# Attention feeding eight routed experts on one core: expert pieces one half-block earlier, the tail's transpose in its own batch, masks and GpSimd fills in another order

## The chip, the core and the metric

The kernel runs on one core of a Trainium2 chip. The core has a matrix engine (PE, with its weight loads counted apart as PEld), a vector engine (DVE), a scalar engine (ACT), GpSimd (POOL) and a queue engine (SP) that issues transfers; POOL issues some transfers too. Each engine takes its instructions in the order in which the program gives them and waits at each for what it reads. The metric is the time of one execution in microseconds (us) on the device; the time of a kernel is the median of its runs.

## The reference

Attention for 8 batches of 8 heads, 576 positions, head size 64, with a causal window of 128 and a slope per head; then a layer of 8 experts whose weights come from eight rounds of row and column scaling.

```python
scores = scale * np.matmul(q, k.transpose(0, 1, 3, 2))
mask = (rel >= 0) & (rel < window)
scores = np.where(mask, scores + bias[None], -1000000000.0)
...
return np.matmul(attn, v)
...
logits = x @ w_gate
P = np.exp(logits - logits.max())
for _ in range(8):
    P /= P.sum(1, keepdims=True) + 1e-09
    P /= P.sum(0, keepdims=True) + 1e-09
    P *= N / E
for e in range(E):
    h = np.maximum(x @ w1[e], 0.0)
    out += P[:, e:e + 1] * (h @ w2[e])
```

x is the attention output, 4608 tokens by 512; the expert weights are 512 by 1024 and 1024 by 512.

## The kernel before

The program has three stretches. In the first, attention runs batch after batch. A batch has 576 positions, cut into five blocks: four full ones of 128 and a tail of 64. Each block is worked in two half-blocks of four heads each, so a batch has ten half-blocks, numbered `at` = 0 to 9 in the code (`at = 2 * kb + u`). A step of the main loop (from L689) works on one half-block: it issues the score products of coming half-blocks (`scores`, L433), the exponential of the next half-block on ACT (`exps`, L439), the mask product of the next one on DVE (`masks`, L444: the exponentials times a table that holds slope and window), and the value product of its own half-block (`values`, L467), followed on DVE by a reciprocal and a division (L477, L478) that leave the block's x. Score products are issued for two half-blocks at once, in odd half-blocks and in the last one of the batch before.

Between these PE does the first two experts' work on batches that are already through attention. A `Filler` holds that work as pieces: an L1 piece (four products at L117, then a ReLU on ACT at L129) counts 0.87 us, an L2 piece (eight products at L141, then a cast on DVE at L554) counts 1.74 us. Each step takes pieces worth `budget`, which is the backlog divided by the half-blocks that are left (`left`, L692); the first is taken ahead of the value product (`filler.fill(1.0)`, L730), the rest behind it (L740). `filler.ready` says how many blocks of x may be used. All products of a unit of four blocks need those four blocks turned.

Turned means that the contracted index lies on the partitions. For batches 0 to 2 and 7, x is turned by PE and copied back; for batches 3 to 6 it is turned by a transposing transfer on the SP queue (`turn_x`, L518). q and k of batches 3 to 7 are turned by transposing transfers of the batch before (`turn_qk`, L313), from half-precision copies made on DVE, POOL and ACT (`cast_qk`), and put in order on DVE and POOL (`order_qk`, L324). The tail's q and k come in one tile: POOL casts it (L331) and SP turns it (L332) into the third tile of `QKT`, which the score products of the fourth block read first.

SP issues in program order: loads of v (L386, for a later block), of q and k (L282, 1 MB each), of the tail (L271), stores of x (L493) and of expert results (L540), and all these transposes. POOL casts v to half precision (`cast_v`, L396), fills the ones that give the softmax sums (L399) and the empty half of a tail block (L398), builds the masks of the block that meets the tail (`tail_masks`, L246 to L248), copies k in order, and issues the expert weight loads.

In the second stretch, after the last batch, the gates' products (L526), the maximum, the exponential and the eight rounds of scaling run on DVE, while PE goes on with expert pieces. In the third stretch experts 2 to 7 are worked, with products that save one in eight of the multiplications; it starts at about 330 us and is not touched by the change.

The lines that set the amount of expert work in a step:

```python
left = (11 - at) % 10 + 1 if b > XPE else 12 - at if b == XPE else 10 - at + 9 * (at == 9)
budget = filler.backlog() / left
...
got = filler.fill(1.0) if b else 0.0
if nxt and nxt[1] < NKB - 1:
    masks(*nxt)
values(b, kb, u)
filler.fill(budget - got)
if at == 1 and b > XPE:
    filler.ready = 4 * b
```

XPE is 3, NKB is 5.

Of the kernel before, what the change touches and what calls it, by code (L numbers as in the profile page):

```python
# [9 lines left out]
FP16 = mybir.dt.float16  # L10
# [4 lines left out]
def kernel(  # L15
# [10 lines left out]
    nc = tc.nc  # L26
# [4 lines left out]
    B, H, S, Dh = q.shape  # L31
    HD = H * Dh
# [3 lines left out]
    P = 128  # L36
# [47 lines left out]
    wg_sb = per.tile([P, NDT, E], FP16, name="wg_sb")  # L84
# [86 lines left out]
    XPE, YO, XSB = 3, 7, 12  # L171
# [59 lines left out]
    asb = first_pool.enter_context(tc.tile_pool(name="asb", bufs=1))  # L231
    sps = first_pool.enter_context(tc.tile_pool(name="sps", bufs=1, space=bass.MemoryType.PSUM))
    if True:
# [10 lines left out]
        def tail_masks():  # L244

            nc.gpsimd.memset(mask[TL:P, :, 0:TL], 0.0)  # L246
            nc.gpsimd.tensor_copy(out=mask[0:TL, :, 0:TL], in_=mask[0:TL, :, P : P + TL])
            nc.gpsimd.tensor_copy(out=mask[:, :, TL:P], in_=mask[:, :, 2 * P : 2 * P + TL])  # L248
# [15 lines left out]
        def spin_alone(n):  # L264
            spins[0] += 1
            spin(aps.tile([P, GT], FP32, name=f"psJ_{spins[0]}", tag="pmm", bufs=4), n)
# [21 lines left out]
        def cast_qk(b, j, which=(1, 0), pool=False):  # L288

            if b not in c16s:  # L290
                c16s[b] = per.tile([P, 2, RI, H, Dh], FP16, name=f"c16_{b}", tag="a8", bufs=8)
            for n in which:
                src = raw[b][n][:, 2 * j : 2 * j + 2, :].rearrange("p h (i d) -> p i h d", i=RI)
                to = c16s[b][:, n, :, 2 * j : 2 * j + 2, :]
                if pool:
                    nc.gpsimd.tensor_copy(out=to, in_=src)
                elif n == 0:
                    nc.vector.tensor_copy(out=to, in_=src)
                else:
                    nc.scalar.copy(out=to, in_=src)  # L300
# [20 lines left out]
        def order_qk(b, n, js):  # L321

            for j in js:
# [2 lines left out]
                    in_=KT[b][:, n, :, j, :].rearrange("p i r -> p r i"),  # L326
                )

        def turn_tail(b):
            t16 = asb.tile([P, HD], FP16, name=f"t16_{b}", tag="xsb", bufs=XSB)  # L330
            nc.gpsimd.tensor_copy(out=t16, in_=tails.pop(b).rearrange("p h d -> p (h d)"))  # L331
            nc.sync.dma_start(out=QKT[b][2][:, :, 0:P], in_=t16, transpose=True)  # L332

        def load_first():
# [57 lines left out]
        def cast_v(m):  # L392
            b, kb = divmod(m, NKB)
            vt = asb.tile([P, H, Dh + 2], FP16, name=f"v_{b}_{kb}", tag="v", bufs=6)
            nk = P if kb < NKB - 1 else TL
            nc.gpsimd.tensor_copy(out=vt[0:nk, :, 0:Dh], in_=v32s.pop((b, kb))[0:nk])  # L396
            if nk < P:
                nc.gpsimd.memset(vt[nk:P], 0.0)  # L398
            nc.gpsimd.memset(vt[0:nk, :, Dh : Dh + 2], 1.0)  # L399
            vs[b, kb] = vt  # L400

        def cols(b, which, j, hb, kb, blocks=1):
# [39 lines left out]
        def masks(b, kb, u):  # L442
            pt = pts[b, kb, u]
            nc.vector.tensor_tensor(out=pt, in0=pt, in1=mask_of[kb][:, 4 * u : 4 * u + 4, :], op=ALU.mult)  # L444
# [113 lines left out]
        for b0 in range(RI, NBLK, 4):  # L558
            order += [(0, b0, 4), (1, b0 - 4, 4)]
        order.append((1, NBLK - 4, 4))  # L560
        filler = Filler(
            (*unit, lambda unit=unit: unit_atoms(*unit, aps, ("pmm", "pmm"), (4, 4), keep))
            for unit in order
        )
# [92 lines left out]
        cast_v(0)  # L657
        load_weights(0, 0, 1)
        cast_v(1)
        cast_v(2)  # L660
        nc.gpsimd.dma_start(out=wg_sb, in_=moe_w_gate.rearrange("(dt p) e -> p dt e", p=P))


        steps = [(b, kb, u) for b in range(B) for kb in range(NKB) for u in range(2)]
        for j in range(2):
# [4 lines left out]
            turn_pe(0, 1, j)  # L670
            turn_pe(0, 0, j)
        tail_masks()
        cast_v(3)
        cast_v(4)
        for j in (2, 3):
# [13 lines left out]
        for n, (b, kb, u) in enumerate(steps):  # L689
            nxt = steps[n + 1] if n + 1 < len(steps) else None  # L690
            at = 2 * kb + u
            left = (11 - at) % 10 + 1 if b > XPE else 12 - at if b == XPE else 10 - at + 9 * (at == 9)  # L692
            budget = filler.backlog() / left
            if b == 0:
                budget = 0.0
            if nxt:
                if nxt[0] < XPE and nxt[1:] == (RI - 2, 1):
                    turn_pe(nxt[0], 0, NDT)
                if nxt == (1, 0, 0):
                    filler.ready = RI  # L700
                    spin_alone(6)
                    for _ in range(NFT):
                        filler.take()
                    cast_qk(1, 0)
                    cast_qk(1, 1)
                    for j in range(NDT):
                        turn_pe(1, 1, j)
                        turn_pe(1, 0, j)
                        if j < 2:
                            cast_qk(1, j + 2, (1,))  # L710
                        filler.take()
                if nxt == (2, 0, 0):
                    filler.fill(8.5)
                    cast_qk(2, 0)
                    cast_qk(2, 1)
                    filler.fill(2.5)
                    for j in range(NDT):
                        turn_pe(2, 1, j)
                        turn_pe(2, 0, j)
                        if j < 2:  # L720
                            cast_qk(2, j + 2, (1,))
                        filler.fill(1.0)
                if n == 0:
                    scores(*nxt)
                elif nxt[2] == 0 and nxt[1] < NKB - 1:
                    scores(*nxt)
                    scores(*nxt[:2], 1)
                if nxt[1] < NKB - 1:
                    exps(*nxt)
            got = filler.fill(1.0) if b else 0.0  # L730
            if nxt and nxt[1] < NKB - 1:
                masks(*nxt)
            if (b, kb, u) == (1, 1, 0):
                spin_alone(8)
            values(b, kb, u)
            if n > 0 and u == 0 and by_pe(steps[n - 1][0]):
                turn_x(*steps[n - 1][:2])
            if u == 1 and n // 2 + NKB < B * NKB:
                cast_v(n // 2 + NKB)
            filler.fill(budget - got)  # L740
            if at == 1 and b > XPE:
                filler.ready = 4 * b
            if at < 8 and b < XPE:
                filler.ready = 4 * b + at // 2
            if at == 8 and b < XPE:
                filler.ready = 4 * b + 4
            if u == 1 and not by_pe(b):
                turn_x(b, kb)
            if u == 1:
                if kb == 1 and b > 0:  # L750
                    gates(4 * b - 4, 4 * b)
                if n // 2 + NKB + 1 < B * NKB:
                    load_v(n // 2 + NKB + 1)
            if b == 0 and at == 5:
                load_weights(1)
            if (b, at) == (1, 8):
                filler.allowed.add(1)
            if (b, at) == (1, 5):
                for j in (2, 3):
                    cast_qk(2, j, (0,), True)  # L760
            if (b, at) == (1, 2):
                filler.hold = False
            if (b, at) == (0, 9):
                load_qk(2, 2)
            if (b, at) == (0, 7):
                homes(1)
            if (b, at) == (1, 3):
                homes(2)
            if 1 <= b < B - 2 and at == 3:
                load_qk(b + 2)  # L770
            if XPE <= b + 1 < B - 1 and at >= 8:
                cast_qk(b + 2, at - 8, (1,), True)
                cast_qk(b + 2, at - 8, (0,))
            if XPE <= b + 1 < B:
                if at == 0 and b + 1 == XPE:
                    for j in range(2):
                        cast_qk(b + 1, j, (1,), True)
                        cast_qk(b + 1, j, (0,))
                if at < 2:
                    cast_qk(b + 1, at + 2, (1,), True)  # L780
                    cast_qk(b + 1, at + 2, (0,))
                if at == 1:
                    store(1)
                    turn_qk(b + 1)
                    order_qk(b + 1, 1, range(NDT))
                if at == 5:
                    turn_tail(b + 1)
                if at in (6, 7):
                    order_qk(b + 1, 0, range(2 * at - 12, 2 * at - 10))
            if b < B - 1 and at == (1 if b > 1 else 5) and b:  # L790
                load_tail(b + 1)
            if 10 * b + at >= 66:
                i = 10 * b + at - 66
                if i % 8 == 0:
                    home_last(2 + i // 8)
                (load_w2 if i % 8 < 4 else load_w1)(2 + i // 8, i % 4, 4)
            if (b, at) == (7, 0):
                todo += sums_of(2, *extras(2))
            if b == 7 and at >= 5:
                some(1)  # L800
# [305 lines left out]
        while filler.l1 or filler.todo or len(filler.l2) > 3:  # L1106
            got = filler.fill(0.9)
# [143 lines left out]
```

## Time and profile before

| what | value |
|---|---|
| median of three runs | 1007.09 us |
| the three runs | 1006.34, 1007.09, 1010.34 us |
| time of the profiled execution | 1010.98 us |
| span of the profiled execution | 1009.2 us |
| mean granted PE clock | 0.998 |
| PE busy 0 to 50 us | 42.6 us |
| PE busy 50 to 285 us | 229.5 us |
| transposing transfers of x, issue to landing | 2.3 least, 3.4 median, 8.5 most |
| transposing transfers of the tail, issue to landing | 4.9 least, 5.7 median, 6.7 most |

A row of a timeline gives the start and the duration in us, the engine, the line, the operation, what it writes and reads, how many, and in brackets how long the engine had been idle and what it waited for. A row of stretches gives from and to, then for each engine the busy time and the number of instructions, the granted PE clock as a share of full speed, the share of the transfer engines and GB/s. An entry of the waits gives the engine and line, what it waited for, the sum in us, how often, and the longest.

### The profile page before, as it was taken

To read this page: it belongs to the slowest core of one execution; us is meant where nothing else is said; L and a number is where in the kernel's file an instruction comes from. 1 tells how busy PE (TensorE), PEld (TensorE's weight loads), DVE (VectorE), ACT (ScalarE), POOL (GpSimd) and SP (SyncE) were. 2 spreads that over 40 slices of the span, in tenths; PEclk is the share of its full clock that TensorE was granted. 3 is DMA by queue.
4 is the path that set the end of the run, shared out by engine and by line. 5 is a ranking of instruction groups with operands and counts; after the bars stand their busy time and mean duration, and the time that the engine had idled before them with its cause. 6 is when DMAs were issued, how large, how long until landed. Compare 5 with 4: busy or idle time off the path is not lost.

```text
span 1009.2 us, 27982 instructions
## 1 busy us (share of the span) xinstructions
PE 992.1 (98%) x11591; PEld 802.0 (79%) x11591; DVE 760.0 (75%) x1598; ACT 717.9 (71%) x1216; POOL 102.5 (10%) x182
## 2 busy tenths in 40 slices
PE   7999999999999999999999999999999999999998
PEld 5745444444544799999999999999999999999997
DVE  5737677565588989877887887887887787787787
ACT  7654554544334668888888888888888888888885
POOL 3314243426110000000000000000000000000000
PEclk9999999999999999999999999999999999999999
DMA  9998789989998335324333334334424333333361
GB/s 241 233 254 215 156 214 221 217 184 170 223 210 162 74 64 96 74 64 96 74 65 96 76 67 97 83 61 95 86 69 81 90 73 72 96 76 68 96 116 48
DMA packets 264431, 122.46 MB, mean 121 GB/s; under 512 B 201968, under 2 KB 255728, under 8 KB 264304
## 3 DMA queue, kind: packets, MB, share of 16 engines
q1 hardware_dynamic: 249568, 102.68, 45.1%
q0 software_dynamic: 14304, 17.84, 10.6%
q8 instruction: 90, 1.47, 0.6%
q14 instruction: 37, 0.30, 0.1%
q10 hardware_dynamic: 432, 0.16, 0.1%
HBM read 78.30 MB, written 23.59 MB: 101 GB/s over the span
## 4 chain that ended last, share of the span: by engine, by line
PE 81%; DVE 3%; DMA 2%; ACT 0%; issue 0%; SPq 0%; DVEq 0%
PE psM L1022 31%; PE psB L985 14%; PE psA L985 9%; PE psC L985 9%; PE psh L117 8%; PE psy L141 7%; DMA xT<-xsb 2%; PE psN L467 1%; PE psS L433 1%; PE psh L964 0%; DMA s5y<-ysp 0%; DVE acc L1066 0%; DVE hs L1168 0%; DVE yo L554 0%; DVE acc L1042 0%
## 5 line engine op out<-in xcount | busy, mean ns | idle before, releaser
L1022 PEld LDWEIGHTS <-hs 128*128 128x128 f16 x2996 | 271.0, 98 | 22.4 <-DVE hs L1002 0.4
L1022 PE MATMUL psM<-w2l,hs 128*128 128x256 f16 x1440 | 186.6, 273 | 0.2 <-DVE hs L1002 0.2
L985 PEld LDWEIGHTS <-w1l 128*128 128x128 f16 x2848 | 181.4, 98 | 4.9 <-issue 0.5
L998 ACT ACTIVATE hs<-hs 128x512 f16<-128x512 f16 x212 | 130.3, 629 | 34.9 <-DVE hs L1168 25.8
L129 ACT ACTIVATE hT<-psh 128x512 f16<-128x512 f32 (+1 forms) x144 | 84.1, 586 | 98.4 <-PE psh L117 98.3
L1168 DVE TENSOR_TENSOR hs<-psB,s5y 128x512 f16<-128x512 f32 x106 | 73.4, 692 | 98.6 <-ACT xs L894 92.4
L985 PEld LDWEIGHTS <-s 128*128 128x128 f16 x2136 | 141.7, 98 | 6.4
L117 PE MATMUL psh<-xT,w1t 128*128 128x512 f16 (+1 forms) x608 | 139.3, 370 | 3.1 <-DMA xT<-xsb 2.8
L894 ACT ACTIVATE xs<-xtok,L_sb 128x512 f16<-128x512 f16 x204 | 136.0, 720 | 2.6 <-DMA xset<-xs 2.5
L141 PE MATMUL psy<-w2t,hT 128*128 128x512 f16 x576 | 135.1, 379 | 0.0
L1022 PE MATMUL psM<-more,hs 128*128 128x256 f16 x864 | 129.5, 273 | 0.0
L985 PE MATMUL psA<-xset,w1l 128*128 128x128 f16 x1424 | 108.6, 219 | 0.0
L985 PE MATMUL psB<-xset,s 128*128 128x128 f16 x1424 | 108.5, 219 | 0.0
L141 PEld LDWEIGHTS <-hT 128*128 128x128 f16 x576 | 53.4, 98 | 60.3 <-issue 2.7
L117 PEld LDWEIGHTS <-w1t 128*128 128x128 f16 x608 | 55.6, 99 | 55.6 <-issue 3.5
L439 ACT ACTIVATE pt<-psS 128x1024 f16<-128x1024 f32 x64 | 64.1, 1022 | 43.4 <-PE psS L433 35.5
L554 DVE CAST yo<-psy 128x512 f16<-128x512 f32 x65 | 44.7, 691 | 59.3 <-PE psy L141 58.0
L1002 DVE TENSOR_TENSOR hs<-hs 128x1024 f16<-128x1024 f16 x107 | 73.9, 691 | 19.7 <-ACT hs L998 17.6
L1159 ACT COPY psC<-psB 128x512 f32<-128x512 f32 x106 | 60.4, 570 | 38.8 <-PE psB L985 38.8
L1151 ACT COPY s5y<-psC 128x512 f32<-128x512 f32 x106 | 62.2, 587 | 22.3 <-PE psC L985 22.3
L1066 DVE TENSOR_TENSOR acc<-acc,psM 128x256 f32<-128x256 f32 (+1 forms) x162 | 73.9, 503 | 0.3
L1147 ACT COPY psB<-psA 128x512 f32<-128x512 f32 x106 | 60.8, 573 | 18.4 <-PE psA L985 18.4
(127 smaller groups left out, 1406.4 us busy)
## 6 DMA issues: line engine op xcount, KB each, us to landing
s5y<-ysp SPq DMA_DIRECT2D x36, 256.0 KB, 3.0
ysp<-yo SPq DMA_DIRECT2D x65, 128.0 KB, 3.3
v<-in_v_dram SPq DMA_DIRECT2D x32, 256.0 KB, 4.7
out_dram<-acc SPq DMA_DIRECT2D x31, 256.0 KB, 2.5
q<-in_q_dram SPq DMA_DIRECT2D x5, 1024.0 KB, 7.8
k<-in_k_dram SPq DMA_DIRECT2D x5, 1024.0 KB, 10.3
xtok<-xd SPq DMA_DIRECT2D x34, 128.0 KB, 2.2
w2t<-in_moe_w_dram POOLq DMA_DIRECT2D x4, 1024.0 KB, 11.0
```

The source lines that it names most:

```text
L117: nc.tensor.matmul(out=ps[:, 0:nt], lhsT=w1ts[e][:, dt, P * ft : P * ft + P], rhs=xT[:, at : at + nb, dt, :], start=(dt == 0), stop=(dt == ...
L129: nc.scalar.activation(out=st["hT"][:, ft, 0:nt], in_=ps[:, 0:nt], func=AF.Relu)
L141: nc.tensor.matmul(out=ps, lhsT=st["hT"][:, ft, P * ms : P * ms + P], rhs=w2ts[e][:, ft, :], start=(ft == 0), stop=(ft == NFT - 1),)
L439: nc.scalar.activation(out=pt, in_=ps.rearrange("p a y n -> p (a y) n"), func=AF.Exp, scale=scale)
L894: nc.scalar.mul(out=xs[2 * (n % 2) + m], in_=xtok[m], mul=P_sb[:, blk, e : e + 1])
L985: nc.tensor.matmul(out=ps[:, j, :], lhsT=q[k][:, P * j : P * j + P], rhs=xset[n % 2][:, x, P * k : P * k + P], start=(start and j == 0 and ...
L998: nc.scalar.activation(out=h[n][:, slot], in_=src, func=AF.Relu)
L1002: nc.vector.tensor_tensor(out=t[:, 4:6], in0=t[:, 0:2], in1=t[:, 2:4], op=ALU.add)
L1022: nc.tensor.matmul(out=Ms[bk][:, half, :], lhsT=h[n][:, LEFT[m], f, :], rhs=W2L[e][RIGHT[m]][:, f, :], start=(e == 2 and f == 0 and half = ...
L1066: nc.vector.tensor_tensor(out=a, in0=a, in1=p2, op=op)
L1151: nc.scalar.copy(out=s5, in_=pc)
L1168: nc.vector.tensor_tensor(out=h[n][:, 3], in0=pb, in1=s5, op=ALU.add)
```

## The change

Four edits. The expert pieces of a batch are spread over half-blocks 1 to 9 and the next batch's 0, where they were spread over 2 to 9 and the next batch's 0 and 1 (from batch 4 on; batch 3's budget is made to end in the same place). The tail's cast stays in half-block 5 of the batch before, into a tile of its own, and its transpose goes to half-block 0 of the batch that reads it. The mask product of the next half-block is issued ahead of the step's first expert piece. On GpSimd a v tile's fills are issued ahead of its cast, and at the start the tail masks go ahead of the third v cast and the load of the gate weights.

```diff
+        t16s: dict = {}
+
+        def cast_tail(b):
+            t16s[b] = asb.tile([P, HD], FP16, name=f"t16_{b}", tag="t16", bufs=1)
+            nc.gpsimd.tensor_copy(out=t16s[b], in_=tails.pop(b).rearrange("p h d -> p (h d)"))
+
         def turn_tail(b):
-            t16 = asb.tile([P, HD], FP16, name=f"t16_{b}", tag="xsb", bufs=XSB)
-            nc.gpsimd.tensor_copy(out=t16, in_=tails.pop(b).rearrange("p h d -> p (h d)"))
+            t16 = t16s.pop(b)
             nc.sync.dma_start(out=QKT[b][2][:, :, 0:P], in_=t16, transpose=True)
...
-            nc.gpsimd.tensor_copy(out=vt[0:nk, :, 0:Dh], in_=v32s.pop((b, kb))[0:nk])
             if nk < P:
                 nc.gpsimd.memset(vt[nk:P], 0.0)
             nc.gpsimd.memset(vt[0:nk, :, Dh : Dh + 2], 1.0)
+            nc.gpsimd.tensor_copy(out=vt[0:nk, :, 0:Dh], in_=v32s.pop((b, kb))[0:nk])
...
-        cast_v(2)
-        nc.gpsimd.dma_start(out=wg_sb, in_=moe_w_gate.rearrange("(dt p) e -> p dt e", p=P))
...
         tail_masks()
+        cast_v(2)
+        nc.gpsimd.dma_start(out=wg_sb, in_=moe_w_gate.rearrange("(dt p) e -> p dt e", p=P))
         cast_v(3)
...
-            left = (11 - at) % 10 + 1 if b > XPE else 12 - at if b == XPE else 10 - at + 9 * (at == 9)
-            budget = filler.backlog() / left
+            left = ((10 - at) % 10 + 1) if b >= XPE else 10 - at + 9 * (at == 9)
+            budget = filler.backlog() / (11 if (b, at) == (XPE, 0) else left)
...
-            got = filler.fill(1.0) if b else 0.0
             if nxt and nxt[1] < NKB - 1:
                 masks(*nxt)
+            got = filler.fill(1.0) if b else 0.0
...
-            if at == 1 and b > XPE:
+            if at == 0 and b >= XPE:
+                turn_tail(b)
+            if at == 0 and b > XPE:
                 filler.ready = 4 * b
...
                 if at == 5:
-                    turn_tail(b + 1)
+                    cast_tail(b + 1)
```

## The prediction

> **What bounds the kernel now.** I read four views in this order: the page's busy times, the waits of PE between 50 and 285 us, the stretches around the longest of them, and the SP and DVE timelines ahead of it.
>
> ```profile
> PE 992.1 (98%) x11591; PEld 802.0 (79%) x11591; DVE 760.0 (75%) x1598; ACT 717.9 (71%) x1216; POOL 102.5 (10%) x182
> ...
> PE psh L117 <- DMA xT<-xsb: 2.8, 2, 2.3
> PE psN L467 <- DVE pt L444: 1.9, 3, 1.2
> PE psN L467 <- DVE xsb L478: 0.2, 1, 0.2
> PE psh L117 <- DVE xsb L478: 0.2, 1, 0.2
> ```
>
> TensorE is the bound: 17 us idle in 1009. About 7.4 us of it lie before 50 us (busy 7.26, 7.98, 7.80, 9.71, 9.87 in the first five stretches of 10), where this change moves only GpSimd work. From 50 to 285 us 5.5 us are left (busy 229.54 of 235), and the list names 5.1 of them: an expert product waiting for turned x (2.8), a value product waiting for masked scores (1.9), slots (0.4). That is all the change can win directly.
>
> ```profile
> 240.57 0.29 PE L467 MATMUL psN<-v,pt 128*128 128x65 f16 x4
> 243.18 1.89 PE L117 MATMUL psh<-xT,w1t 128*128 128x512 f16 x4 [2.32 <-DMA xT<-xsb]
> ...
> 228.40 0.59 SPq L386 DMA_DIRECT2D v<-in_v_dram  x1
> 232.72 1.23 SPq L332 DMA_TRANSPOSE tT<-t  x1
> 233.99 0.57 SPq L540 DMA_DIRECT2D ysp<-yo  x1
> 234.66 1.44 SPq L518 DMA_TRANSPOSE xT<-xsb  x1
> ...
> 243.00:243.50 0.50, 0.32 (x1) 0.13 (x2) 0.21 (x1) 0.00 (x0) 0.00 (x0) 0.58 1.10 257
> 243.50:246.00 2.50, 2.50 (x17) 1.47 (x16) 0.42 (x2) 0.60 (x1) 1.83 (x4) 0.50 1.06 325
> 246.50:247.00 0.50, 0.50 (x4) 0.20 (x2) 0.02 (x1) 0.00 (x0) 0.50 (x2) 1.00 0.99 76
> ```
>
> The longest wait, 2.32 us, is at the start of batch 7. In front of it the SP queue stands from 229.0 to 232.7 because the tail's transpose (L332) waits for GpSimd's cast; behind it stands the turn of batch 6's last full block (L518), issued at 234.66 and landing after 8.5 us, at 243.1. The wait costs twice: the granted clock (third figure from the right) is 0.5 until about 246.45, 3.4 us at half speed, so 1.7 us more. Together 4.0 us.
>
> ```profile
> 121.77 1.02 ACT L439 ACTIVATE pt<-psS 128x1024 f16<-128x1024 f32 x1
> ...
> 123.67 0.69 DVE L554 CAST yo<-psy 128x512 f16<-128x512 f32 x1 [2.28 <-PE psy L141]
> ...
> 124.28 1.59 DVE L444 TENSOR_TENSOR pt<-pt,mask 128x1024 f16<-128x1024 f16 x1
> ...
> 125.92 0.39 PE L467 MATMUL psN<-v,pt 128*128 128x65 f16 x7 [1.16 <-DVE pt L444]
> ```
>
> Here the mask product's input is there at 122.8, but VectorE stands 2.28 us at the cast of an expert piece that PE has not finished; the mask comes after it, and is stretched from 0.68 to 1.59 while GpSimd copies. PE then waits 1.16 us.
>
> **The change, part by part.**
>
> *Masks in front.* Nothing is added; one 0.68 us VectorE instruction changes places with the piece's 0.69 us cast. In the row above the mask can start at 122.8 and is done before 124.4, ahead of its reader (124.58). The idles of this kind are 0.36 at 83.25, 1.16 at 125.92 and 0.42 at 208.75; slot waits are 0.17 at 120.20 and 0.22 at 163.00. The wait added: VectorE now waits for the exponential ahead of the cast, and behind it stand the cast and the value half-block's reciprocal. The cast's slot is one of four, asked for again four allocations later, over 3 us of PE work, against at most 0.7 us of delay. Bounds: 2.33 us gained, or all of it handed on to the next wait. That next wait is worked out below.
>
> *Work a half-block sooner.* Half-block numbers run 0 to 9 in a batch. A batch from 4 on has 27.8 us of expert pieces (16 of 0.87, 8 of 1.74). By the budget lines, before, they run in half-blocks 2 to 9 and 0 and 1 of the next; after, in 1 to 9 and 0. Nothing is added to PE, but the first product of a batch now stands ahead of the value product of half-block 1 (0.24 us of PE), so it asks for the turned x 0.24 us sooner on the clock. Counted from the value product that makes that block (half-block 7), old: five L1 pieces, four L2, two score groups, four value groups, 13.3 us. New: two L1 (1.73), four L2 (6.92), two score groups (1.08), values 0.85: 10.6 us. So 2.7 us of cover is gone, and the turn must make it up.
>
> *Tail turned later.* The transposes per batch are as many as before. L332 leaves half-block 5 and goes to half-block 0 of the next batch. In its old place it took 2.59 us at 135.04, 3.44 at 166.99, 2.67 at 200.43 and, with its wait, 4.95 from 229.0; the last L518 stands right behind it with one store between. In its new place the queue is less filled; the smallest row is 1.23, and that lands on the load, turn and stores ahead of the next q/k transposes (L313), which SP reaches at 149.9, 182.7 and 215.9 with no slack. So those come 1.2 us later, and the last L518 comes 1.4 to 3.7 us sooner. GpSimd's cast is cast_tail at the old place, in its own tile, so nothing of POOL is moved past; its reader, the score group of half-block 5, is over 10 us behind the new issue against 4.9 to 6.7 us to landing.
>
> What this leaves, batch by batch. Batch 4: old PE was free at 139.89 and waited 0.50. New it is free at 139.89 - 1.69 (three idles before) - 0.24 = 137.96. L518 goes into the slot of L332 at 135.04, whose landing took 4.9: 139.9. The new wait is about 2.0, so of 2.2 us of idle only 0.2 is won; a turn landing like the quickest (2.3) would leave none, so 0.2 to 2.2. I take 0.2, since the row is the same queue slot. Batches 5 and 6 landed at 173.86 (PE free at 173.85) and 206.8 (free at 207.15); with L518 1.4 us or more sooner, no wait, and the 0.64 at 163.00 and 208.75 is won. Batch 7: the value product is 10.6 us before a need at about 239.8, so at 229.2; x is ready 2.6 later as before (227.19 to 229.82), issue 231.8, landing after 3.4 (median) or 8.5 (longest): 235.2 to 240.3. I take no wait: 4.0 won; at worst 0.5 is left.
>
> *The end of attention.* The old budget leaves two L2 pieces: one covers the way from the last turn on PE (275.35) over VectorE's copy to the gates (277.31). The new one leaves one, which goes ahead of the turn; behind it nothing is ready. Cast 0.69 and copy 0.28 then lie open: about 0.9 us of idle. From the gates on, the pieces of the Sinkhorn part come out the same.
>
> *GpSimd.* Fills first: 0.11 us (0.64 for tail blocks) leaves the way from a landed v to its product, which shows in PE's waits only at 22.81 (1.33 us, v landing at 21.6): 0.1 at most. Tail masks (2.24 us) go ahead of the third v cast, which ends at about 16.8 instead of 16.5; its product is at 18.40. Cover is 1.6 us, and if it were gone the wait at 22.81 would take it in. Zero, within 0.3 either way.
>
> Those mask copies then run beside mask products at 14.97 and 16.12 instead of 18.12, where a product took 0.87 against 0.68; 0.2 either way. [...]
>
> **Sum** for the profiled execution: -4.0 - 0.2 - 0.6 + 0.9 = -3.9, so 1010.98 to 1007.1. But the three runs are 1006.34, 1007.09 and 1010.34: two lie about 4.0 below the profiled one, the very price of wait and slow clock. I take it that the median run has a shorter wait there, without the slow clock: between 0 and about 1.5 us (the longest PE idle that left the clock at 1.00 is 1.33). With half of that, 0.7, the median gains 0.7 + 0.2 + 0.6 - 0.9 = 0.6, and some of batch 4's upper bound of 2.2: about 1 us, **1006.0**.
>
> What a gap does to the clock decides much: 1.33 us did nothing, 2.32 halved it, and batch 4's new wait of 2.0 lies between. [...]
>
> **Rivals.**
> - *All waits go, and the 4 us were in the unprofiled runs as well.* For it: the offset may be the profiling. Against: two levels among the runs themselves. 1007.09 - 4.0 - 2.2 - 0.6 + 0.9 = 1001.2. Chance 0.14.
> - *The turn lands late at several batch starts* (slower). If L518 lands over 2 us after the need, each start costs 2.3 + 1.7. It decides where the 2.7 us of lost cover is more than the queue gives back. For it: turns that took 6.9 to 8.5 us to land behind the q/k loads. Against: SP, not PE, set the time of issue. Two such starts and the gap at the end: 1007.1 + 8.0 + 0.9 = 1016. Chance 0.12.
> - *Nothing at the batch starts, one slow clock in batch 4, and the gap at the end:* 1007.1 + 1.7 + 0.9 = 1009.7. Chance 0.16.
>
> **Numbers.** The forecast has 0.58. Within 0.5% (5 us, about what a measurement tells from no change) lie it and the third rival: 0.74; faster 0.14, slower 0.12. The range 1001.5 to 1011 leaves out the slower rival and about half of the first, 0.19.
>
> **What would show it.** Right: no SP wait ahead of the tail's transpose, no 0.5 clock at the start of batch 7, a PE wait of 1 to 2 us near 138 to 140, about 0.9 us of idle before the gates, no wait of L467 on L444 after 50 us. Wrong: DMA waits of L117 over 2 us at several batch starts, or q/k copies that keep score groups waiting.

## The result

| | before | after |
|---|---|---|
| median of 21 runs each | 1007.29 us | 1004.33 us |
| lowest and highest | 1005.95, 1011.46 us | 1003.84, 1008.59 us |
| profiled execution: time, span | 1010.98, 1009.2 us | 1004.29, 1002.5 us |
| mean granted PE clock of the profiled execution | 0.998 | 1.000 |

The ratio of the times is 0.9969, with a 95% interval of 0.996 to 0.9978: about 3 us faster, or 0.3%. 1006.0 was forecast, 1.7 us above what came.

The busy times of the page after the change:

```profile
PE 989.1 (99%) x11591; PEld 801.5 (80%) x11591; DVE 762.1 (76%) x1598; ACT 717.8 (72%) x1216; POOL 104.7 (10%) x182
```

PE's waits between 50 and 285 us after the change (sum, times, longest):

```profile
PE psh L117 <- DMA xT<-xsb: 2.5, 2, 1.3
PE psX L510 <- DVE xsb L483: 0.3, 1, 0.3
```

No wait for a mask is left, and none of 2.3 us. In its place stand two waits for a turned x of 1.27 and 1.23 us. The line numbers are five higher than before in this part: the x transposes are L523 (were L518), the tail's L337 (L332), mask products L449 (L444), value products L472 (L467), stores of expert results L545 (L540), gates L531 (L526).

Most of the difference lies between the first L1 product of batch 1 that follows the warm-up (52.02 before, 50.99 after) and the last gates' products (277.31 and 270.65). The stretch between the two, before:

```profile
52.02:277.31 225.29, 219.84 (x1738) 109.64 (x1737) 136.01 (x290) 111.80 (x161) 79.53 (x135) 0.99 0.93 206
```

and after:

```profile
50.99:270.65 219.66, 216.75 (x1737) 109.19 (x1735) 137.93 (x290) 111.35 (x161) 82.30 (x134) 1.00 0.92 212
```

The stretch is 5.63 us shorter: 2.54 of PE idle (5.45 to 2.91) and 3.09 of PE busy, of which the half clock of batch 7 is 1.7; what the other 1.4 are isn't traced. From the gates to the end both take the same (731.89 and 731.85). The other 1.0 us of the two profiles' difference is there already at the first value product (13.05 and 12.06), whose v landed that much sooner in the one execution; none of the experiments ties it to the change.

Three places show what became of the steps. PE's timeline after the change, at the start of batches 4 and 6 and at the end of attention (start, duration, line, what it writes and reads, how many; in brackets the idle time before and what ended it):

```profile
136.22 0.61 PE L438 MATMUL psS<-qN,kN 64*128 64x256 f16 x8
138.10 1.04 PE L117 MATMUL psh<-xT,w1t 128*128 128x512 f16 x4 [1.27 <-DMA xT<-xsb]
...
205.13 1.02 PE L117 MATMUL psh<-xT,w1t 128*128 128x512 f16 x4 [1.23 <-DMA xT<-xsb]
...
237.96 1.04 PE L117 MATMUL psh<-xT,w1t 128*128 128x512 f16 x4
...
270.43 0.29 PE L510 MATMUL psX<-ident,xsb 64*128 64x64 f16 x4
270.65 1.08 PE L531 MATMUL psG<-wg_sb,xT 128*128 128x8 f16 x32
```

Batch 7's first product (237.96) follows without idle. The gates start 0.22 us after the start of the last turn on PE.

SP's queue after the change:

```profile
132.89 1.88 SPq L545 DMA_DIRECT2D ysp<-yo  x1
134.87 1.22 SPq L523 DMA_TRANSPOSE xT<-xsb  x1
...
198.50 3.27 SPq L523 DMA_TRANSPOSE xT<-xsb  x1
...
228.31 1.21 SPq L523 DMA_TRANSPOSE xT<-xsb  x1
...
239.59 1.52 SPq L337 DMA_TRANSPOSE tT<-t  x1
```

The turn that batch 7 needs goes out at 228.31, with no tail's transpose ahead of it, and lands at 233.76; the tail follows at 239.59. Batch 4's turn goes out at 134.87, directly behind a store of 1.88 us. Batch 6's, at 198.50, holds the queue for 3.27.

DVE after the change, in the place where a mask product of 1.59 us was shown:

```profile
121.58 0.69 DVE L559 CAST yo<-psy 128x512 f16<-128x512 f32 x1 [0.38 <-PE psy L141]
122.98 1.08 DVE L449 TENSOR_TENSOR pt<-pt,mask 128x1024 f16<-128x1024 f16 x1 [0.70 <-ACT pt L444]
```

The mask product now starts when its exponential is there (122.94), and PE doesn't wait for it.

### The profile page after: what moved, and what is told of

Its sections match the earlier page's. It is cut to its first block, busy times and chain, and to the rows that moved or that the text cites. A ratio compares the mean times of both kernels' runs of the same rounds, so it can differ in the third digit from the quotient of the medians.

```text
span 1002.5 us, 27939 instructions
## 1 busy us (share of the span) xinstructions
PE 989.1 (99%) x11591; PEld 801.5 (80%) x11591; DVE 762.1 (76%) x1598; ACT 717.8 (72%) x1216; POOL 104.7 (10%) x182
## 4 chain that ended last, share of the span: by engine, by line
PE 91%; DMA 3%; DVE 3%; ACT 1%; issue 0%; SPq 0%; POOL 0%; DVEq 0%
PE psM L1029 31%; PE psB L992 14%; PE psh L117 12%; PE psy L141 11%; PE psA L992 9%; PE psC L992 9%; DMA v<-in_v_dram 2%; PE psN L472 1%; PE psS L438 1%; DMA xT<-xsb 1%; PE psT L368 1%; DVE pt L449 0%; DMA q<-in_q_dram 0%; PE psG L531 0%; PE psh L971 0%
## 5 line engine op out<-in xcount | busy, mean ns | idle before, releaser
L444 ACT ACTIVATE pt<-psS 128x1024 f16<-128x1024 f32 x64 | 64.5, 1021 | 58.1 <-PE psS L438 57.6
L449 DVE TENSOR_TENSOR pt<-pt,mask 128x1024 f16<-128x1024 f16 x64 | 49.2, 769 | 40.7 <-ACT pt L444 40.7
```

What stands on the lines that cost most here:

```text
L444: nc.scalar.activation(out=pt, in_=ps.rearrange("p a y n -> p (a y) n"), func=AF.Exp, scale=scale)
```

## The experiments

Ten variants, one of them measured twice (all_but_sooner and old_budget_again are the same kernel), and the whole change once more, in three groups; the kernels of a group share a chip and the runs of the kernel before. The measured values of all of them:

| kernel | masks | sooner | tail | GpSimd | median, us | before in its group | ratio, 95% interval | runs with a mean PE clock under 0.999 | PE waits for turned x / for masks in its profile, us |
|---|---|---|---|---|---|---|---|---|---|
| masks_alone | x | | | | 1006.56 | 1007.72 | 0.9996 (0.9984 to 1.0007) | 3 of 11 | 2.2 / 0 |
| sooner_alone | | x | | | 1006.04 | 1007.72 | 0.9987 (0.9974 to 1.0000) | 4 of 12 | 1.9 / 0.4 |
| tail_alone | | | x | | 1006.56 | 1007.72 | 0.9990 (0.9979 to 1.0001) | 0 of 11 | 0 / 2.0 |
| gpsimd_alone | | | | x | 1007.24 | 1007.72 | 1.0006 (0.9993 to 1.0019) | 4 of 12 | 2.1 / 2.0 |
| all_but_tail | x | x | | x | 1006.85 | 1008.52 | 0.9988 (0.9975 to 1.0002) | 7 of 12 | 2.1 / 0 |
| all_but_sooner | x | | x | x | 1004.63 | 1008.52 | 0.9958 (0.9943 to 0.9974) | 0 of 5 | 1.8 / 0.2 |
| all_but_gpsimd | x | x | x | | 1006.17 | 1008.52 | 0.9975 (0.9961 to 0.9988) | 5 of 12 | 1.6 / 0 |
| middle | x | in part | x | x | 1005.37 | 1008.52 | 0.9965 (0.9953 to 0.9978) | 4 of 12 | 2.9 / 0.3 |
| full_again | x | x | x | x | 1005.06 | 1007.61 | 0.9978 (0.9966 to 0.9990) | 4 of 12 | 1.6 / 0 |
| old_budget_again | x | | x | x | 1004.44 | 1007.61 | 0.9968 (0.9955 to 0.9980) | 0 of 6 | 0.4 / 0 |
| masks_and_tail | x | | x | | 1004.58 | 1007.61 | 0.9968 (0.9957 to 0.9979) | 0 of 8 | 0.9 / 0 |
| sooner_and_tail | | x | x | | 1004.47 | 1007.61 | 0.9966 (0.9954 to 0.9978) | 0 of 5 | 1.8 / 0.4 |

The 21 runs of the change itself have the lowered mean clock in 5, the kernel before in 19 of the 83 runs of the three groups. Such runs are 1 to 4 us longer than the others of their kernel (medians before, in the three groups: 1009.01, 1010.12 and 1009.45 against 1007.01, 1008.05 and 1007.34). One stretch of 3.41 us at half clock, as in the profile before (243.09 to 246.50), makes the mean of a run of 1005 us 0.998; by this estimate such a run has at least one, but its mean doesn't say where: in the profile of middle it is at 9.3 us, far ahead of batch 4. Some waits for turned x stand in the traces under the name of another instruction that had long been done: those of all_but_tail and all_but_gpsimd at batch 4, and one of 0.71 in masks_alone at batch 7 (239.64). In each the turn landed 0.04 to 0.09 us before the product started. masks_and_tail has 1.2 us more in three waits of value products for a slot. The profile of all_but_sooner is of an execution of 1007.61 us, 3 us above its kernel's median, at the full clock.

### Each part by itself

Masks in front, and nothing else:

```diff
-            got = filler.fill(1.0) if b else 0.0
             if nxt and nxt[1] < NKB - 1:
                 masks(*nxt)
+            got = filler.fill(1.0) if b else 0.0
```

> The kernel before with only the mask product put ahead of the step's first expert piece. Theory A (the gain comes from the SP queue, which no longer stands at the tail's transpose): no wait of the value product on the mask product is left after 50 us, but the turned x of batch 4 is then waited for instead, and the wait and slow clock at batch 7 stay: 0 to 1.0 us faster. Rival B (the gain is masks and GpSimd order, 1.7 us of mask waits): 1.5 to 2 us faster.

Pieces a half-block sooner, and nothing else:

```diff
-            left = (11 - at) % 10 + 1 if b > XPE else 12 - at if b == XPE else 10 - at + 9 * (at == 9)
-            budget = filler.backlog() / left
+            left = ((10 - at) % 10 + 1) if b >= XPE else 10 - at + 9 * (at == 9)
+            budget = filler.backlog() / (11 if (b, at) == (XPE, 0) else left)
...
-            if at == 1 and b > XPE:
+            if at == 0 and b > XPE:
                 filler.ready = 4 * b
```

> The kernel before with only the expert pieces moved one half-block earlier; the tail's transpose stays in half-block 5 of the batch before. Theory A: the cover of the last turn is 2.7 us shorter and nothing gives it back, so PE waits for turned x at every start of batches 4 to 7, 0.5 to 4 us each, with the slow clock at least at batch 7: 1 to 5 us slower. Rival B (turns are early enough anyway): within 1 us of before.

The tail's cast in its own tile, its transpose in its own batch, and nothing else:

```diff
+            if at == 0 and b >= XPE:
+                turn_tail(b)
...
                 if at == 5:
-                    turn_tail(b + 1)
+                    cast_tail(b + 1)
```

> The kernel before with only the tail's transpose moved to half-block 0 of its own batch (its cast stays). Theory A: the SP queue no longer stands at 229 us, the last turn is issued 1.4 us or more sooner, no wait for turned x from batch 5 on and no slow clock at batch 7: about 2.5 to 3 us faster, most of what all four edits gave. Rival B: within 1 us of before.

GpSimd's order, and nothing else:

```diff
-            nc.gpsimd.tensor_copy(out=vt[0:nk, :, 0:Dh], in_=v32s.pop((b, kb))[0:nk])
...
             nc.gpsimd.memset(vt[0:nk, :, Dh : Dh + 2], 1.0)
+            nc.gpsimd.tensor_copy(out=vt[0:nk, :, 0:Dh], in_=v32s.pop((b, kb))[0:nk])
...
-        cast_v(2)
-        nc.gpsimd.dma_start(out=wg_sb, in_=moe_w_gate.rearrange("(dt p) e -> p dt e", p=P))
...
         tail_masks()
+        cast_v(2)
+        nc.gpsimd.dma_start(out=wg_sb, in_=moe_w_gate.rearrange("(dt p) e -> p dt e", p=P))
```

> The kernel before with only GpSimd's order changed (fills ahead of casts; at the start the tail masks ahead of the third v cast). Theory A: within 0.5 us of before; the 1.0 us that the profile after is ahead at 50 us was there at its first value product (12.06 against 13.05 us) and is how the first loads happened to land. Rival B: 1 us faster, with the first 32 L1 products of 512 columns at about 51.0 us instead of 52.0.

Measured: no part alone is worth more than 0.13%, and only sooner_alone's interval ends at 1 rather than above it. masks_alone and gpsimd_alone came in time as their theories A had it, though the profile of masks_alone has no slow clock at batch 7. tail_alone was to give 2.5 to 3 us, most of the gain, and gave about 1: that theory fell. The traces show why two of them win so little. With the masks in front alone, every mask wait is gone, and the first products of batches 4 and 7 wait instead. PE in masks_alone:

```profile
140.03 1.04 PE L117 MATMUL psh<-xT,w1t 128*128 128x512 f16 x4 [1.52 <-DMA xT<-xsb]
...
239.64 1.02 PE L117 MATMUL psh<-xT,w1t 128*128 128x512 f16 x4 [0.71 <-DVE rden L477]
```

and in sooner_alone:

```profile
140.10 1.02 PE L117 MATMUL psh<-xT,w1t 128*128 128x512 f16 x4 [1.86 <-DMA xT<-xsb]
```

Batch 4's product starts at 140.0 to 140.1 in both, against 140.4 in the kernel before (139.89 and 0.50 of wait): PE comes sooner, the transfer doesn't. The theory under which the pieces alone make the kernel 1 to 5 us slower fell: batch 4 waited, but at batch 7 SP had the tail's transpose issued at 229.10, x's turn went out at 230.43 and landed at 236.70, 1.9 us ahead of the product (238.63), so no wait arose there.

With the tail alone, it is the other way round. PE's waits of tail_alone between 50 and 275 us:

```profile
PE psN L472 <- DVE pt L449: 2.0, 4, 0.9
PE psN L472 <- POOL v L404: 0.7, 2, 0.4
PE psh L117 <- DVE xsb L483: 0.2, 1, 0.2
```

No product waits for a turned x, and the mask waits stay. GpSimd's order is worth nothing that can be measured. Its profile has the wait of batch 7 and its price again. PE in gpsimd_alone:

```profile
241.03 1.04 PE L117 MATMUL psh<-xT,w1t 128*128 128x512 f16 x4 [2.15 <-DMA xT<-xsb]
```

From that product to the gates it takes 34.28 us, and 34.13 in the kernel before, where the clock was halved too. In masks_alone, masks_and_tail and old_budget_again, with the same budget and the full clock, the way is 32.50, 32.67 and 32.66. So the half clock costs 1.5 to 1.8 us, as forecast (1.7).

How long batch 7 waits, with the tail in its old place, hangs on GpSimd, one link further back than the prediction followed it. GpSimd in the kernel before:

```profile
225.33 4.87 POOL L324 COPY kN<-qk 128x512 f16<-128x512 f16 x4 [10.29 <-DMA qk<-c]
...
232.08 0.61 POOL L331 CAST t<-t 128x512 f16<-128x512 f32 x1
```

and in masks_alone:

```profile
221.13 4.57 POOL L324 COPY kN<-qk 128x512 f16<-128x512 f16 x4 [8.61 <-DMA qk<-c]
...
227.58 1.06 POOL L331 CAST t<-t 128x512 f16<-128x512 f32 x1
```

The tail's cast is queued behind the copies of k, which wait for the q/k transposes. Those went out at 215.94 in the one and at 213.00 in the other; the tail's transpose left SP 4.0 us sooner in the second, x's turn at 230.61 instead of 234.66, and batch 7 waited 0.71 us for x instead of 2.32. PE itself was 1.9 us further on in the second (its need at 238.93 and 240.86), so 2.1 us of the 4.0 are the chain's own: 1.0 by when SP reached the q/k transposes, the rest by how they landed. So the wait of batch 7 was no fixed price in the kernel before. The tail's move takes the chain out of the turn's way altogether.

### Each part left out, and a budget in between

The tail left as it was:

```diff
             if at == 5:
-                cast_tail(b + 1)
+                turn_tail(b + 1)
...
-            if at == 0 and b >= XPE:
-                turn_tail(b)
```

> The changed kernel with the tail's transpose put back to half-block 5 of the batch before. Theory A (three edits each take their own PE waits, and the tail's place is what keeps the turned x early): waits for turned x of 1.5 us or more at batch 4 and one of the later batches, the slow clock in a fifth of the runs or more; 1 to 2 us faster than the kernel before, so 1 to 2 us behind the full change. Rival C (with the pieces a half-block sooner, the SP queue is not held up by the tail any more, so its place is worth nothing): 2.5 to 3.5 us faster than before, as the full change.

The old budget:

```diff
-            left = ((10 - at) % 10 + 1) if b >= XPE else 10 - at + 9 * (at == 9)
-            budget = filler.backlog() / (11 if (b, at) == (XPE, 0) else left)
+            left = (11 - at) % 10 + 1 if b > XPE else 12 - at if b == XPE else 10 - at + 9 * (at == 9)
+            budget = filler.backlog() / left
...
-            if at == 0 and b > XPE:
+            if at == 1 and b > XPE:
                 filler.ready = 4 * b
```

> The changed kernel with the expert pieces' budget put back (half-blocks 2 to 9, 0 and 1). Theory A: no wait for turned x over 0.5 us and none of the value product on the mask; no slow clock; 1.5 to 2.5 us faster than before. Rival C (the sooner pieces are the larger part): under 1.5 us faster.

GpSimd's old order (fills behind the cast, `cast_v(2)` and the load of the gate weights ahead of `tail_masks()`):

```diff
-            nc.gpsimd.memset(vt[0:nk, :, Dh : Dh + 2], 1.0)
             nc.gpsimd.tensor_copy(out=vt[0:nk, :, 0:Dh], in_=v32s.pop((b, kb))[0:nk])
+            nc.gpsimd.memset(vt[0:nk, :, Dh : Dh + 2], 1.0)
```

> The changed kernel with GpSimd's order put back. Theory A: GpSimd's order is worth nothing: 2.5 to 3.5 us faster than the kernel before. Rival: it gave up to 1 us of the gain: 1.5 to 2.5 us faster.

The old budget, but the new batch's pieces let in in half-block 1, behind its value product:

```diff
-            if at == 1 and b > XPE:
-                filler.ready = 4 * b
...
+            if at == 1 and b > XPE:
+                filler.ready = 4 * b
+                budget += filler.backlog() / 11
             filler.fill(budget - got)
```

> A version of its own: masks, tail and GpSimd as in the changed kernel, the budget as before, but the new batch's pieces are let in between: half-block 1 begins with the last old L2 piece, as before the change, and only its second lot, behind the value product, takes the new batch's L1 pieces. The first use of turned x is 1.7 to 2 us later than in the changed kernel. Theory A: no wait for turned x over 0.5 us at any batch, no slow clock, 3.5 to 4.5 us faster than before, ahead of the full change. Rival C: the waits for turned x in the changed kernel (1.27 and 1.23 us) are slack that returns elsewhere; 2.5 to 3.2 us faster, as the full change.

Measured: without the tail's move the gain falls to 0.12%; without the pieces' move it is 0.42%, the largest of all; without GpSimd's order 0.25%. Of these only the first two have intervals that lie apart, by 0.0001. all_but_tail came in time and clock as theory A had it, with one batch start waiting and not two. all_but_sooner was to be 1.5 to 2.5 us faster by theory A and under 1.5 by its rival; it gave about 4, with waits of 0.84 and 0.93 at batches 4 and 6 where none over 0.5 was to be: both missed. The 0.25% without GpSimd's order lies between its two theories. The budget in between gains 0.35%, but the waits for turned x that its theory excluded are there (1.52 at 141.90 and 1.35 at 176.26), so it doesn't settle where the pieces cost. PE in all_but_tail, at batch 4:

```profile
138.91 1.04 PE L117 MATMUL psh<-xT,w1t 128*128 128x512 f16 x4 [2.06 <-DVE pt L444]
```

That is the two waits handed to one place: masks gone, pieces sooner, and the tail's transpose still ahead of the turn. In this profile the clock stayed at 1.00; 7 of the kernel's 12 runs have the lowered mean.

### Pairs, and the whole once more

The last group asks whether the tail with one partner does as much as all four. For old_budget_again the first range of the text is meant to read 0.9955 to 0.997.

> The whole change once more, beside the three below and the same runs of the kernel before. Theory L (the tail's later turn and the masks in front carry the gain, the pieces a half-block sooner give part of it back, through the turned x of batches 4 and 6 and a slow clock in a quarter of the runs): 0.997 of before, mean granted clock .998 or less in about a quarter of the runs, waits for turned x of 1.0 to 1.3 us at batches 4 and 6. Rival W (the whole is what counts, the parts only add noise): the same 0.997, and the masks and tail kernels within 0.1% of it.

> Everything but the pieces' half-block, a second time. Theory L: 0.955 to 0.967 hundredths off one, that is 0.9955 to 0.967 + 0.03 = 0.997 at the most, 0.05 to 0.15% under the whole change, and no run, or one in ten, with a mean granted clock of .998. Rival W: 0.997, equal to the whole change within 0.05%, with the slow clock as often as there.

masks_and_tail is the kernel before with the first and the third of the diffs shown for single parts, sooner_and_tail with the second and the third:

```diff
+            if at == 0 and b >= XPE:
+                turn_tail(b)
...
             if nxt and nxt[1] < NKB - 1:
                 masks(*nxt)
+            got = filler.fill(1.0) if b else 0.0
```

> Masks in front and the tail turned later, GpSimd's order and the budget as before. Theory L: each alone gave 0.9996 and 0.9990; together with the slow clock gone and both kinds of waits gone 0.996 to 0.9975, no slow clock; equal to the kernel with GpSimd's order within 0.1%. Rival G (GpSimd's order carries a part once the waits are gone): 0.9985, the sum of the two alone, and so 0.2% or more above the kernel with GpSimd's order.

```diff
-            if at == 1 and b > XPE:
+            if at == 0 and b >= XPE:
+                turn_tail(b)
+            if at == 0 and b > XPE:
                 filler.ready = 4 * b
```

> Pieces a half-block sooner and the tail turned later, masks and GpSimd's order as before. Theory L: the sum of the two alone is 0.9977, the mask waits (about 2 us) stay, the slow clock comes in a quarter of the runs: 0.998, above masks and tail by 0.1% or more. Rival S (the earlier half-block carries the gain once the tail is out of its way): 0.9970 or less, not above masks and tail.

Measured: 0.9966 to 0.9968 for all three that are not the whole change, and 0.9978 for the whole. old_budget_again and masks_and_tail came as theory L had it; full_again had the lowered clock in 4 of 12, and waits of 0.62 and 0.97 at batches 4 and 6 where 1.0 to 1.3 were expected. The theory that GpSimd's order carries a part fell (0.9968 with it and without). The theory that the pieces give something back missed on sooner_and_tail: 0.998 was expected, 0.9966 came, as its rival S had it, and the mask waits it was to keep were 0.4 us, not 2. The pieces' move takes most mask waits away by itself: 0.4 in the two kernels that have it with the old order of masks, 1.9 to 2.0 in those that have neither. How they do so wasn't traced. So masks and pieces win the same microseconds, the tail others, and the tail with either of the two gives about what all four give. Alone the parts give 0.04, 0.13 and 0.10%, masks with tail 0.32%. That is more than the sum, and the traces fit it: masks or pieces alone hand what they win to the turned x of batch 4, and the tail alone leaves the mask waits. The intervals, 0.1% to either side, don't show it by themselves.

What the pieces do beside the tail shows in the queue. SP in old_budget_again:

```profile
131.82 0.60 SPq L391 DMA_DIRECT2D v<-in_v_dram  x1
132.52 2.58 SPq L523 DMA_TRANSPOSE xT<-xsb  x1
```

With the new budget the store of an expert result (L545, 132.89 in the rows of after) stands between the load of v and this turn, so the turn goes out 2.35 us later by the clock; it does so in full_again and sooner_and_tail too (134.00 and 134.06, turns at 135.93 and 136.20). But the turn that goes out sooner holds the queue for 2.58 us instead of 1.22, and lands only 0.74 us sooner (137.32 against 138.06), so of the 2.35 us of delay 0.7 reach PE. PE's waits of old_budget_again, 50 to 280 us:

```profile
PE psh L117 <- DMA xT<-xsb: 0.4, 1, 0.4
```

Batch 4's wait is 0 to 0.87 in the four profiles that have the tail's move and the old budget, and 0.62 to 1.80 in the four that have both moves. The stretch up to the gates is the shortest in old_budget_again:

```profile
51.43:268.57 217.14, 216.79 (x1737) 108.87 (x1736) 135.39 (x290) 111.78 (x161) 81.03 (x134) 1.00 0.95 216
```

0.35 us of idle is left in 217. Its profiled span of 1000.3 is the shortest seen.

Of the lowered clock the runs say this: none of 30 runs of the three kernels with the tail's move and the old budget has it; of the kernels with masks, pieces and tail it is 14 of 45 (the change's 21, all_but_gpsimd, full_again), about as often as before the change. In the runs without it, the whole change (1004.61) is level with the pairs (1004.45 to 1004.58). sooner_and_tail had it in none of 5, too few to say. That longer waits at batch 4 bring it back is likely, but not shown: none of the three profiles of the whole change and of all_but_gpsimd caught it, and the one lowered profile of a kernel with the tail's move, middle's, has it at the start of the program.

Dropping the pieces' move is thus the version that the runs favour: 0.9958 and 0.9968 of before in two groups, against 0.9969 and 0.9978 for the whole change. The intervals of the two overlap, so that it beats the whole change isn't shown in the median; in the clock it is 0 of 11 runs against 14 of 45. masks_and_tail and sooner_and_tail are level with it, and nothing here chooses between the three.

## Why the prediction was right, and where it was off

**Batch 7's wait goes, with the half clock behind it: right.** The turn goes out at 228.31 instead of 234.66, the product doesn't wait, and the clock stays at 1.00. The issue came 3.5 us sooner than the forecast 231.8, because the value product came at 227.19 and not 229.2, and the turn 1.1 us behind it and not 2.6. tail_alone's profile, with this edit alone, has no wait there either; those of sooner_alone and all_but_tail, with the tail in its old place, have none too, so it is the 30 runs without a lowered clock, more than the one profile, that speak for the tail's move. The price of the clock was right as well (1.7; 1.5 to 1.8 measured).

**Masks in front: right in the trace, their worth misjudged.** The waits went as named. That they would be handed on to batch 4 was forecast, and masks_alone shows it. Not foreseen was that the pieces' move alone takes most of them.

**Batch 4, a new wait of about 2.0 at 138 to 140: right in place, mis-sized.** It was 1.27 at 138.10. The issue was forecast at 135.04 and came at 134.87; it landed after 3.2 us instead of 4.9. A second execution gave 0.62. That a wait of 2.0 costs no half clock, as the sum has it, was the author's estimate. No profile has a wait of just that length; in this one the clock stays at 1.00 after the 1.27, as it does after 1.80 in sooner_and_tail, 1.86 in sooner_alone and 2.06 in all_but_tail, while in gpsimd_alone it is halved after 2.15.

**Batches 5 and 6, no wait: wrong for 6.** The step that failed is "with L518 1.4 us or more sooner, no wait". The turn was issued 5.3 us sooner (198.50 against 203.81), but held the queue for 3.27 us, as the tail's transpose had held it in that place (2.67), and landed only 1.8 us sooner (205.0 against 206.8); PE was 3.2 us ahead of its old place by then (203.9 against 207.15). Price 1.23 us, and 0.97 in full_again. It is not tied to the pieces alone: all_but_gpsimd and sooner_and_tail have no wait there, and all_but_sooner has one of 0.93.

**The end of attention, 0.9 us of idle: mis-sized.** The way from the last turn over the cast and the copy was taken as open in full. The gates' products start 0.22 us behind the start of that turn and take 1.08: only the last of the eight blocks that they read needs the last copy, and the others cover it. PE shows no idle there; from the turn to the next expert product it takes 1.17 us (270.43 to 271.60), against 1.03 before (275.35 to 278.11, less 1.73 for the L2 piece between). So the price is about 0.1 us.

**The q/k transposes 1.2 us later: wrong.** They went out at 148.43, 181.15 and 213.75, 1.5 to 2.2 us sooner than before (149.9, 182.7 and 215.9), where DVE's reciprocals of half-block 1 came 1.9 to 2.4 us sooner.

**2.7 us less cover: right, and of no weight at batches 5 and 7.** What the budget changed at batch 4 was a place in SP's queue, not only the time of need; the prediction counted PE's work and not the store that the work puts ahead of the turn.

**GpSimd zero: right**, within 1.0006 and its interval.

**From the profiled execution to the median: the size that was off.** 0.6 us came out of the terms and about 1 was forecast; in the runs without the lowered clock the change measures 2.7 (1004.61 against 1007.34 in the last group). Half of 1.5 us had been taken as batch 7's wait in a median run, since 1.33 was the longest idle that had left the clock alone. The experiments have waits of 1.86 and 2.06 with the clock at 1.00, so a run of the kernel before can wait 2 us there without the half clock. With 2.0 for it, the terms are 2.0 + 0.9 (batch 4: 2.2 less 1.27) - 0.6 (batches 5 and 6: 0.64 less 1.23) - 0.1 (the end) = 2.2 by the waits of the change's profile, and 2.0 + 1.6 - 0.3 - 0.1 = 3.2 by those of full_again. So the mis-sized term is batch 7's wait in a run without the half clock, and after it batch 4's. The first of these is argued: no profile caught the kernel before without the half clock. That the time fell inside the range is in part the range's width: the gain was nearly three times the forecast one, and the idle put down for the end (0.9) and the wait left out at batch 6 (1.2) largely offset each other. That most runs of before don't have the half clock was right: 64 of 83.

**The rivals.** All waits go: no, 0.9969 is short of it (1001.2 was its time). The turn lands late at several batch starts: its mechanism came, at batches 4 and 6, with 1.2 us each and no half clock, so below the 2 us from which it was to decide. One slow clock in batch 4: not in the profiles.

## What to carry to other kernels

Where one resource is busy 98% of the time and short waits are left, edits that each remove a wait may remove the same one, or hand it to the next; try pairs before adding parts up, and undo each part of what works, since here one of four gave nothing and another may be better left out. A transfer's place in the issue queue was part of its cost: with the pieces a half-block sooner a store of 1.88 us stood ahead of batch 4's turn, which went out 2.35 us later and landed 0.74 us later, so look at whose transfer the store of a moved piece gets ahead of. And one profiled execution can be the dear one, as here (1010.98 us against a median of 1007.29): look at how the granted clock is spread over the runs before a wait from the profile is priced for the median.

## What the runs showed of the hardware

**The clock was halved for 3.4 us after PE gaps of 1.71 to 2.32 us in three profiled executions, and stayed at 1.00 after gaps of 1.80 to 2.06 in three others.** It was halved after gaps of 2.32 (before), 2.15 (gpsimd_alone) and, at the start of the kernel, 1.71 (middle). Waits of 1.80 (sooner_and_tail), 1.86 (sooner_alone) and 2.06 us (all_but_tail) left it at 1.00. Stretches of gpsimd_alone, ahead of and in the half clock (from and to, length, busy time of PE, weight loads, DVE, ACT, POOL, the granted clock, the share of the transfer engines, GB/s):

```profile
238.70:242.11 3.41, 1.26 (x16) 0.67 (x14) 2.40 (x5) 0.00 (x0) 0.14 (x1) 1.00 1.56 251
242.11:245.50 3.39, 3.37 (x18) 1.54 (x15) 0.94 (x3) 1.19 (x2) 3.39 (x7) 0.50 0.73 171
```

of middle, ahead of it:

```profile
5.93:9.34 3.41, 1.50 (x19) 1.02 (x17) 1.12 (x2) 2.24 (x6) 0.00 (x0) 1.00 1.07 331
```

and of all_but_tail, around the wait of 2.06 us (136.84 to 138.91) that did nothing:

```profile
134.63:138.04 3.41, 2.21 (x20) 1.06 (x17) 3.34 (x10) 1.02 (x1) 0.50 (x1) 1.00 1.18 230
138.04:141.46 3.42, 2.55 (x16) 1.26 (x17) 1.80 (x4) 1.09 (x2) 2.17 (x5) 1.00 0.57 169
```

The clock falls 1.0 to 1.1 us after the gap is over in the first two (products resume at 241.03 and 8.36, half clock from 242.1 and 9.34), and at its very end in the kernel before (243.18 and 243.1). The 3.41 us ahead of the fall hold 1.26, 1.50 and, in the kernel before, 1.19 us of PE work; the two stretches of all_but_tail, which divide its wait, hold 2.21 and 2.55. Gaps of 2.06 and 2.15 us thus cost nothing in one execution and 1.6 to 1.8 us in another.

Two traces show more. In the kernel before, the record of the granted clock begins at 4.15 us, and the fall (243.09) and the rise (246.50) lie 70 and 71 times 3.413 us behind that. Cut into stretches of 3.413 us from there, two full stretches of that execution hold less than 1.78 us of PE work: 1.19 (239.67 to 243.09) and 1.30 (1004.26 to 1007.67, at the end of the program); behind both the clock is 0.50. In the execution after, cut in the same way from 4.00, the least is 1.61 (997.28 to 1000.69, at the end), with the clock at 1.00 behind it, and the next 2.18. That the clock goes by the work in such steps, and that a gap costs something or nothing by where their edges lie in it, is the author's estimate from these figures; no run shows it by moving one against the other. Worked out by it from the two gaps (2.06 and 2.32), with the half clock behind a step of 1.50 us of work or less (middle's) and the edges in all places, the wait of all_but_tail would bring the half clock in about half of them (7 of its 12 runs have it), and that of the kernel before in 56% (19 of 83 have it, so most of its runs would wait less than the profiled one).

**A transposing transfer of x held the SP queue for 1.2 to 3.3 us.** In the profile after, the smallest issue of x's turn is 1.205 us and the longest 3.273; issue to landing is 2.3 to 7.0 us. The longest (198.50) follows another turn that was still under way (195.40, landing at 202.39), but the one at 134.87 does so too and took 1.22, so what makes an issue long isn't shown. Issuing it 5.3 us sooner brought batch 6's landing only 1.8 us forward.
